# Two attention bursts joined into one, four pairs of loads of v reordered, and one difference of h taken later, in a retention and bilinear FFN kernel

## The chip, the cores and the metric

The kernel runs on one core of one Trainium2 chip. The metric is the device time of one execution in microseconds (us); the number that counts is the median over several executions. The profiler records one further execution, and its times are given from the first instruction of that execution (the span's start).

## What is computed

A linear attention with a decay per head (retention), and behind it a feed-forward layer with a product of two branches. The inputs are float32; the kernel works in bfloat16 with sums in float32.

```python
B, H, S, D = 4, 8, 768, 64
gamma = 1 - 2 ** (-5 - arange(H))
for t in range(S):
    state = gamma * state + einsum('bhd,bhe->bhde', k[:, :, t], v[:, :, t])
    y[:, :, t] = einsum('bhd,bhde->bhe', q[:, :, t], state) / sqrt(D)
x = y.transpose(0, 2, 1, 3).reshape(B * S, H * D)         # 3072 x 512
out = ((x @ w_a) * (x @ w_b)) @ w_out                     # 512 -> 1536 -> 512
```

## The kernel before

**Slots.** The attention is done in chunks of 128 positions, called slots: 24 of them, six to a batch. For one slot `t` the decay is multiplied into k and q (`scaled`, one operation each on POOL for slots 6 and up), both go through a transposing DMA on SP's queue (`flip`, L300), `scores(t)` multiplies them on TensorE in quarters of 64 x 64, VectorE multiplies the causal mask on (`aT`, L333), `update(t)` adds the slot to the running state in PSUM and a copy of it goes to `gst`, `inter(t)` multiplies the state with q, `intra(t)` the masked scores with v, and `leave(t)` copies the output y of a pair of slots to `xt` on ScalarE (L386). `turn(new, old)` writes such a burst down: scores and update for the slots `new` and `new+1`, and inter, intra and leave for `old` and `old+1`; either can be None. If both are given, the scores of `new+1` take two of the three "ff" banks of PSUM, else they take the banks y0 and y1.

**Tiles.** The FFN takes tokens in tiles J of 4, 2, 2, 2, 2, 4 and 8 slots. For tile J and each of twelve blocks `ft` of 128 hidden columns, `ffn_a` multiplies x with w_a (four matmuls, L522; ScalarE copies the result to `asb`, L525) and `ffn_g` with w_b (four matmuls, L534; VectorE multiplies `asb` on and writes `ht`, L536). `blocks(J, a, b)` does a and g in turn, `three(J, ft)` does three a's and then three g's. `a` and `g` use the three "ff" banks in rotation: a bank can be written again when its copy or product is through. The third step, h times w_out, is done by a Strassen-Winograd scheme of seven products on sums and differences `hs1` to `hs4` of quarters of `ht`. `single(J, A, B, C)` writes the seven products (`p1` to `p7`, L638) down with the first three blocks of the next tile between them, and A, B, C name the PSUM banks of its three accumulators. `hsum(J, s, a, b, eng)` makes one such sum for the blocks a to b (and a+6 to b+6); `hsums` makes the sums 2, 1 and 4.

**Order.** The order of all work is written out by hand: `seq` chains the instructions of each engine in the order in which the program makes them, and so does SP's queue with its DMAs. `casts(t)` is the step that brings a slot in: on POOL it scales k and q (and converts v, unless t is 12 to 19, whose v ScalarE converts in `v_cast`), and on SP's queue it issues `flip(t)` and then the loads of slot t+2. `load_slot(t)` issues k, then q (for a pair of slots at once, at the even one), then v. `store()` at the start of each block issues the output DMAs held until then, on the same queue.

**Sums of the sixth tile.** Tile 5 has four slots, and its sums are made in pieces: `WHEN` says behind which block which are made. A name such as "346" is sum 3 of blocks 4 to 6. Behind blocks 5 to 7 they run on VectorE, behind 8 and later on POOL.

```python
def turn(new, old, eng=nc.scalar):
    ...
    if new is not None:
        if two or old is None:
            update(new, eng)
        scores(new + 1, "y" if old is None else "ff")
        scores(new, "at")
    if old is not None:
        inter(old)
        inter(old + 1)
    ...
```

Of the kernel before, what the change touches and what calls it, by code (L numbers as in the profile page):

```python
# [16 lines left out]
PAIRS = 3  # L17


LOADS = "p0 p1 w0 w1 a1 b1 a2 k2 q2 b2 v2 o0 o1 o2 o3 o4 o5 s6 t8".split()  # L20


@with_exitstack
def kernel(
# [10 lines left out]
    nc = tc.nc  # L35
# [7 lines left out]
    NFT = DFF // P  # L43
    NSLOT = B * NCH
# [49 lines left out]
    def seq(bi):  # L94
        ins = bi.ins
        prev = last.get(ins.engine)
        if prev is not None:
            tc.add_manual_dep(ins, prev.name, nosync, reason="program order")
        last[ins.engine] = ins
        return bi  # L100
# [4 lines left out]
    def load_slot(t, names="kqv"):  # L105
        b, ci = divmod(t, NCH)
        for nm in names:
            src = {"k": k, "q": q, "v": v}[nm]
            if nm == "q":
                if t % 2 == 0:  # L110
                    load_two(nm, src, b, ci // 2, t)
                continue
            if t % 2 == 0:
                whole[nm] = raw.tile([P, 2, H, D], F32, tag=nm + "f", name=nm + "f")
            raws[nm, t] = whole[nm][:, t % 2]
            s = src[b, :, ci * P : (ci + 1) * P, :].rearrange("h p d -> p h d")
            seq(nc.sync.dma_start(out=raws[nm, t], in_=s))
# [5 lines left out]
    def load_two(nm, src, b, u, t):  # L123
        f = raw.tile([P, H, 2, D], F32, tag=nm + "f", name=nm + "f")
        s = src[b, :, 2 * u * P : 2 * (u + 1) * P, :].rearrange("h (p two) d -> p h two d", two=2)
        seq(nc.sync.dma_start(out=f, in_=s))  # L126
        for par in range(2):
            raws[nm, t + par] = f[:, :, par, :]
# [25 lines left out]

    pending = list(LOADS)

# [78 lines left out]
    def cast(engine, dst, src):  # L235
        if engine is nc.scalar:
            seq(nc.scalar.copy(dst, src))
        else:
            seq(engine.tensor_copy(dst, src))  # L239
# [29 lines left out]
    def scaled(eng, t, i):  # L269
        tab = tabs[0] if i else tabs[1 if t < 2 * PAIRS else 2]  # L270
        dst, src, tab = kqb[t][:, i], raws["kq"[i], t], tab[:, t % NCH]
        if t < 2 * PAIRS:
            dst, src = (x.rearrange("p (hp r) d -> p hp r d", r=2) if x is src else x
                        for x in (dst, src))
            tab = tab.rearrange("p (hp r) o -> p hp r o", r=2).to_broadcast([P, HP, 2, D])
        else:
            dst = dst.rearrange("p hp r d -> p r hp d")
            src = src.rearrange("p (r hp) d -> p r hp d", r=2)
            tab = tab.rearrange("p (r hp) o -> p r hp o", r=2).to_broadcast([P, 2, HP, D])
        seq(eng.tensor_tensor(dst, src, tab, op=ALU.mult))  # L280

    def new_nat(t):
        kqb[t] = nat.tile([P, 2, HP, 2, D], BF16, tag="kqb", name="kqb")
        kb[t], qb[t] = kqb[t][:, 0], kqb[t][:, 1]
        vb[t] = nat.tile([P, H, D], BF16, tag="vb", name="vb")

    def casts(t):
        new_nat(t)
        scaled(nc.gpsimd, t, 0)
        scaled(nc.gpsimd, t, 1)  # L290
        if t not in range(12, 20):
            cast(nc.gpsimd, vb[t], raws["v", t])
        flip(t)
        if t + 2 < NSLOT:
            load_slot(t + 2)

    def flip(t):
        if t % 2 == 0:
            kqT[t // 2] = tra.tile([P, 2, 2, HP, P], BF16, tag="kqT", name="kqT", bufs=3)
        seq(nc.sync.dma_start_transpose(  # L300
            out=kqT[t // 2][:, t % 2].rearrange("p a b c -> p (a b) c"),
            in_=kqb[t].rearrange("p a hp r d -> p (a hp r d)")))
# [19 lines left out]
    def scores(t, where):  # L322
        at = score_banks(where)
        for hp in range(HP):
            for c in range(2):
                for r in range(2):
                    seq(nc.tensor.matmul(at[r][half(c), hp, :],  # L327
                                         kqT[t // 2][half(r), t % 2, 0, hp, half(c)],
                                         kqT[t // 2][half(r), :, 1, hp, half(t % 2)],
                                         start=True, stop=True, skip_group_check=True))  # L330
        aT[t] = tra.tile([P, 2, HP, P], BF16, tag="aT", name="aT")
        for r in range(2):
            seq(nc.vector.tensor_tensor(aT[t][:, r], at[r], mask.to_broadcast([P, HP, P]), op=ALU.mult))  # L333
        psff.back(*at)

    def update(t, eng):
        ci = t % NCH
        if ci == NCH - 1:
            return
        if ci == 0:  # L340
            state[0] = psst.tile([P, HP, D], F32, tag="st", name="st")
        st = state[0]
        for hp in range(HP):
            for r in range(2):
                seq(nc.tensor.matmul(st[half(r), hp, :], kb[t][:, hp, r, :],  # L345
                                     vb[t][:, HP * r + hp, :],
                                     start=(ci == 0 and hp == 0), stop=(hp == HP - 1),
                                     skip_group_check=True))
        cast(eng, gst[(t + 1) % 4], st)
# [39 lines left out]
    def turn(new, old, eng=nc.scalar):  # L389
        if old is not None:  # L390
            ys[old // 2] = [psat.tile([P, 2, 2, 2, P // 2], F32, tag=f"y{r}", name="y") for r in range(2)]
        two = new is not None and (new + 1) % NCH < NCH - 1
# [8 lines that stand above are left out]
        if two:  # L401
            update(new + 1, nc.scalar)
        elif new is not None and old is not None:
            update(new, eng)
        if old is not None:
            intra(old)
            intra(old + 1)
            leave(old)
# [130 lines left out]
    def ffn_ab(J, ft):  # L539
        store()  # L540
        ffn_a(J, ft)
        ffn_g(J, ft)
# [53 lines left out]
    def hsum(J, s, a, b, eng=nc.vector):  # L596
        U = slice(int(J == 0), 2 if isinstance(J, tuple) else TILES[J] // 2)
        hs_tile(J, s)
        v = ht[J].rearrange("p (k j) (u r n) -> p r k j u n", k=2, r=2, n=P)
        A11, A12, A21, A22 = (v[:, r, k2, a:b, U] for r in range(2) for k2 in range(2))  # L600
        S = {x: hs[J, x][:, a:b, U] for x in (1, 2, 3, 4) if (J, x) in hs}
        x, y, op = {3: (A11, A21, ALU.subtract), 2: (A22, S[3], ALU.subtract), 1: (A21, A22, ALU.add),
                    4: (A12, S.get(2), ALU.subtract)}[s]
        tt(S[s], x, y, op, eng)

    def hsums(J, a, b, eng):
        for s in (2, 1, 4):
            hsum(J, s, a, b, eng)

    WHEN = {5: ["302"], 6: ["324"], 7: ["346", "202"], 8: ["102", "402"], 9: ["224", "124"],  # L610
            10: ["424"], 11: ["246", "146", "446"]}

    def sums(J, ft, eng=nc.vector):
        for what in WHEN.get(ft, []):
            hsum(J, *map(int, what), eng)

    class Group:

# [84 lines left out]
    FF = (psff, "ff")  # L703
    Y0, Y1, AT0, AT1 = ((psat, x) for x in ("y0", "y1", "at0", "at1"))
    ST = (psst, "st")

    def single(J, A, B, C):
        g = Group(J, 0, A, B, C)
        g.p1()
        g.p7()  # L710
        g.p2()
        ffn_ab(J + 1, 0)
        g.p6()
        ffn_ab(J + 1, 1)
        g.p5()
        ffn_ab(J + 1, 2)
        g.p3()
        g.p4()
# [239 lines left out]
    V_ = nc.vector  # L958

    def blocks(J, a, b):  # L960
        for ft in range(a, b):
            ffn_ab(J, ft)
            if J == 5 and ft + 1 < b:
                sums(J, ft, G_ if ft > 8 else nc.vector)

    def three(J, ft):
        store()
        for f in range(ft, ft + 3):
            ffn_a(J, f)
        for f in range(ft, ft + 3):  # L970
            ffn_g(J, f)

    def v_cast(t):
        cast(nc.scalar, vb[t], raws["v", t])
# [26 lines left out]
    hsum(2, 3, 0, 6, G_)  # L1001
    blocks(2, 6, 7)
    turn(8, None)
    three(2, 7)
    hsums(2, 0, 3, G_)
    casts(12)
    turn(None, 8)
    blocks(2, 10, NFT)
    hsums(2, 3, 6, G_)
    casts(13)  # L1010
    single(2, Y0, AT0, FF)
    casts(14)
    blocks(3, 3, 4)
    turn(10, None, V_)
    three(3, 4)
    hsum(3, 3, 0, 6, G_)
    v_cast(12)
    blocks(3, 7, 8)
    v_cast(13)
    blocks(3, 8, 9)  # L1020
    casts(15)
    hsums(3, 0, 3, G_)
    blocks(3, 9, 10)
    turn(12, 10)
# [74 lines left out]
```

## Time and profile before

| | us |
|---|---|
| median of 3 runs | 221.0 (220.89 to 221.03) |
| profiled execution, its own time | 221.23 |
| its span, first to last instruction | 219.5 |
| busy: TensorE (PE) | 212.4 |
| busy: GpSimd (POOL) | 142.1 |
| busy: VectorE (DVE) | 139.1 |
| busy: ScalarE (ACT) | 99.3 |

The profiled execution is 0.2 us above the median, and 1.7 us of its time lie outside the span. The granted TensorE clock is full throughout. In a row of the timeline stand the start, the length (both in us), the engine, the line, the operation, what is written and read, how many instructions were merged, and in brackets the idle time before the row with what ended it. The length of a TensorE row runs over the start of the next one, because matmuls overlap; the distance between two starts is what counts. SPq is the sequencer of SP issuing DMAs.

### The profile page before, as it was taken

What the parts mean: (1) busy time and instruction counts of PE and PEld (TensorE: products, weight loads), DVE (VectorE), ACT (ScalarE), POOL (GpSimd) and SP (SyncE); (2) the same over time, 40 slices, a digit from 0 to 9 for tenths busy, and PEclk for the clock granted to TensorE, in tenths of its full rate; (3) what the DMA queues carried; (4) which work ended last, traced back from release to release, by engine and by line L of the source; (5) the groups of instructions that cost most, each with busy time, mean ns of one, the idle gap of its engine ahead of it and who ended that gap; (6) DMA issues with size and microseconds to landing.
All of it is one profiled execution on the core that took longest, in us unless ns stands there. A gap on an engine that the chain in (4) does not pass through costs nothing.

```text
span 219.5 us, 5638 instructions
## 1 busy us (share of the span) xinstructions
PE 212.4 (97%) x2242; PEld 143.6 (65%) x2242; DVE 139.1 (63%) x254; ACT 99.3 (45%) x217; POOL 142.1 (65%) x163
## 2 busy tenths in 40 slices
PE   7789999999999999999999999999999999999994
PEld 3457445687458888888888655456865444448883
DVE  3776346846783463675477246986595787789642
ACT  3256325343234453455576345445545656642331
POOL 5266876778444659669675958999999975520000
PEclk9999999999999999999999999999999999999999
DMA  6999999999999995999999999960022000000055
GB/s 168 290 323 367 384 315 358 379 244 247 221 243 232 275 201 131 217 191 281 174 220 239 218 170 227 266 61 3 4 85 106 0 1 3 0 0 1 27 191 167
DMA packets 85146, 39.68 MB, mean 181 GB/s; under 512 B 57472, under 2 KB 78848, under 8 KB 85120
## 3 DMA queue, kind: packets, MB, share of 16 engines
q1 hardware_dynamic: 84976, 39.26, 76.4%
q8 instruction: 17, 0.28, 0.6%
q10 hardware_dynamic: 144, 0.07, 0.1%
q14 instruction: 9, 0.07, 0.1%
HBM read 28.31 MB, written 6.29 MB: 158 GB/s over the span
## 4 chain that ended last, share of the span: by engine, by line
PE 89%; SPq 3%; DMA 3%; issue 1%; DVE 1%; POOL 0%; ACT 0%; DVEq 0%
PE a L522 19%; PE g L534 19%; PE mA L638 12%; PE uA L778 8%; PE mB L638 6%; PE o L559 5%; PE uB L778 4%; SPq L126 3%; DMA wsta<-in_moe_w_a_dram 3%; PE mC L638 3%; PE at L327 2%; PE uC L778 2%; PE y L375 2%; PE ka L837 2%; PE kb L837 2%; PE st L345 1%
## 5 line engine op out<-in xcount | busy, mean ns | idle before, releaser
L536 DVE TENSOR_TENSOR ht<-g,asb 128x256 bf16<-128x256 f32 (+1 forms) x74 | 36.9, 502 | 37.0 <-PE g L534 32.3
L522 PE MATMUL a<-xt,wa_bf 128*128 128x256 bf16 (+1 forms) x296 | 52.4, 304 | 0.4 <-DVE ht L536 0.2
L534 PE MATMUL g<-xt,wb_bf 128*128 128x256 bf16 (+1 forms) x296 | 52.2, 304 | 0.0
L525 ACT CAST asb<-a 128x256 bf16<-128x256 f32 (+1 forms) x74 | 32.4, 437 | 39.2 <-PE a L522 37.1
L534 PEld LDWEIGHTS <-wb_bf 128*128 128x128 bf16 x296 | 28.6, 98 | 12.6
L522 PEld LDWEIGHTS <-wa_bf 128*128 128x128 bf16 x296 | 27.9, 98 | 13.0 <-DVE xt L239 0.7
L280 POOL TENSOR_TENSOR kqb<-kf,ktab 128x512 bf16<-128x512 f32 x22 | 23.1, 1056 | 16.3 <-DMA kf<-in_k_dram 10.7
L638 PEld LDWEIGHTS <-hs 128*128 128x128 bf16 x240 | 23.3, 98 | 3.9
L333 DVE TENSOR_TENSOR aT<-at,mask 128x512 bf16<-128x512 f32 x36 | 22.3, 681 | 0.3
L784 ACT COPY snap<-uA 128x512 f32<-128x512 f32 x30 | 16.7, 588 | 12.6 <-PE uA L778 12.6
L280 POOL TENSOR_TENSOR kqb<-qf,qtab 128x512 bf16<-128x512 f32 x18 | 19.3, 1071 | 3.0 <-DMA qf<-in_q_dram 3.0
L645 ACT COPY snaps<-mA 128x256 f32<-128x256 f32 x30 | 11.2, 374 | 19.8 <-PE mA L638 19.7
L572 POOL TENSOR_TENSOR hs<-ht,hs 128x384 bf16<-128x384 bf16 (+1 forms) x17 | 16.6, 983 | 5.3 <-DVE ht L536 5.3
L638 PEld LDWEIGHTS <-ht 128*128 128x128 bf16 x180 | 17.5, 98 | 2.8
L572 POOL TENSOR_TENSOR ht<-gsb,asb 128x512 bf16<-128x512 bf16 x12 | 13.6, 1158 | 6.3 <-DVE gsb L572 6.3
L572 POOL TENSOR_TENSOR hs<-ht 128x384 bf16<-128x384 bf16 (+2 forms) x12 | 13.8, 1153 | 4.2 <-DVE ht L536 4.2
L638 PE MATMUL mA<-wsum,hs 128*128 128x256 bf16 x120 | 15.7, 273 | 0.0
L239 POOL CAST vb<-vf 128x512 bf16<-128x512 f32 x16 | 10.3, 657 | 7.5 <-DMA vf<-in_v_dram 7.0
L572 DVE TENSOR_TENSOR osb<-mB,snaps 128x256 f32<-128x256 f32 x20 | 8.4, 422 | 9.1 <-PE mB L638 4.7
L386 ACT CAST xt<-y 128x512 bf16<-128x512 f32 x18 | 9.7, 589 | 2.3 <-PE y L375 2.2
L559 PE MATMUL o<-wo_bf,ht 128*128 128x512 bf16 x48 | 10.7, 379 | 0.0
L572 DVE TENSOR_TENSOR gsb<-uB,snap 128x512 bf16<-128x512 f32 x10 | 6.9, 686 | 4.2 <-ACT snap L784 2.6
(104 smaller groups left out, 327.2 us busy)
## 6 DMA issues: line engine op xcount, KB each, us to landing
qf<-in_q_dram SPq DMA_DIRECT2D x12, 512.0 KB, 5.7
out_dram<-osb SPq DMA_DIRECT2D x21, 256.0 KB, 4.1
kf<-in_k_dram SPq DMA_DIRECT2D x18, 256.0 KB, 4.3
vf<-in_v_dram SPq DMA_DIRECT2D x18, 256.0 KB, 5.2
wsta<-in_moe_w_a_dram SPq DMA_DIRECT2D x6, 512.0 KB, 7.7
wstb<-in_moe_w_b_dram SPq DMA_DIRECT2D x6, 512.0 KB, 8.0
wsto<-in_moe_w_out_dram SPq DMA_DIRECT2D x6, 512.0 KB, 8.9
kf<-in_k_dram SPq DMA_DIRECT2D x3, 512.0 KB, 7.1
```

The source lines that it names most:

```text
L280: seq(eng.tensor_tensor(dst, src, tab, op=ALU.mult))
L333: seq(nc.vector.tensor_tensor(aT[t][:, r], at[r], mask.to_broadcast([P, HP, P]), op=ALU.mult))
L522: seq(nc.tensor.matmul(a, wa_bf[:, kt, fs], xcols(J, kt, c0, c1), start=(kt == 0), stop=(kt == KT - 1)))
L525: seq(nc.scalar.copy(asb, a))
L534: seq(nc.tensor.matmul(g, wb_bf[:, kt, fs], xcols(J, kt, c0, c1), start=(kt == 0), stop=(kt == KT - 1)))
L536: seq(nc.vector.tensor_tensor(ht[J][:, ft, c0:c1], g, asbs.pop((J, ft, c0)), op=ALU.mult))
L559: seq(nc.tensor.matmul(o, ht[J][:, ft, i * P : (i + 1) * P], wo_bf[:, ft], start=(ft == 0), stop=(ft == NFT - 1), skip_group_check=True))
L572: seq(eng.tensor_tensor(dst, x, y, op=op))
L638: seq(nc.tensor.matmul(m, w, right[:, j], start=(first and j == 0), stop=(j == NP - 1), skip_group_check=True))
L645: seq(nc.scalar.copy(self.snaps[:, n], self.bank["A"]))
L778: seq(nc.tensor.matmul(m, w, right[:, k], start=(first and k == 0), stop=(k == 1), skip_group_check=True))
L784: seq(nc.scalar.copy(self.snaps[n], self.bank["A"]))
```

## The change

- The burst `turn(None, 8)` and the burst `turn(10, None, V_)` become one `turn(10, 8)`, which stands behind block 10 of tile 2, ahead of the seven products of tile 2. `update(10)` thereby comes behind the inter products, and the copy of its state is on ScalarE and no longer on VectorE. The `three(3, 4)` that followed the second burst becomes plain blocks.
- `single(2)` has Y1 as its second accumulator's bank and no longer AT0.
- For the slots 12 to 19, v of the even slot is no longer loaded behind q of that slot but behind k of the odd slot, so it stands behind the next transposing DMA in SP's queue.
- `casts(12)` moves ahead of three blocks and of the sums `hsums(2, 0, 3)`; `casts(15)` moves ahead of `hsum(3, 3, 0, 6)`.
- Sum "202" of tile 5 is made behind block 9 and no longer behind block 7, still on VectorE; "402", which reads it, is made behind block 10 and no longer behind block 8, on POOL as before.

```diff
+V_LATE = range(12, 20)
@@ casts
-        if t + 2 < NSLOT:
-            load_slot(t + 2)
+        u = t + 2
+        if u in V_LATE:
+            load_slot(u, "kq")
+            if u % 2:
+                load_slot(u - 1, "v")
+                load_slot(u, "v")
+        elif u < NSLOT:
+            load_slot(u)
@@ sums of tile 5
-    WHEN = {5: ["302"], 6: ["324"], 7: ["346", "202"], 8: ["102", "402"], 9: ["224", "124"],
-            10: ["424"], 11: ["246", "146", "446"]}
+    WHEN = {5: ["302"], 6: ["324"], 7: ["346"], 8: ["102"], 9: ["202d", "224", "124"],
+            10: ["402", "424"], 11: ["246", "146", "446"]}
@@
-            hsum(J, *map(int, what), eng)
+            hsum(J, *map(int, what[:3]), nc.vector if what[3:] else eng)
@@ the written order
     turn(8, None)
+    casts(12)
     three(2, 7)
     hsums(2, 0, 3, G_)
-    casts(12)
-    turn(None, 8)
-    blocks(2, 10, NFT)
+    blocks(2, 10, 11)
+    turn(10, 8)
+    blocks(2, 11, NFT)
     hsums(2, 3, 6, G_)
     casts(13)
-    single(2, Y0, AT0, FF)
+    single(2, Y0, Y1, FF)
     casts(14)
-    blocks(3, 3, 4)
-    turn(10, None, V_)
-    three(3, 4)
+    blocks(3, 3, 6)
+    casts(15)
     hsum(3, 3, 0, 6, G_)
+    blocks(3, 6, 7)
     v_cast(12)
     blocks(3, 7, 8)
     v_cast(13)
     blocks(3, 8, 9)
-    casts(15)
     hsums(3, 0, 3, G_)
     blocks(3, 9, 10)
     turn(12, 10)
```

## The prediction

> **What bounds the kernel now.** I read the page first: busy time and the chain of work that ended last. Then the busy time by stretches.
>
> ```profile
> PE 212.4 (97%) x2242; PEld 143.6 (65%) x2242; DVE 139.1 (63%) x254; ACT 99.3 (45%) x217; POOL 142.1 (65%) x163
> PE 89%; SPq 3%; DMA 3%; issue 1%; DVE 1%; POOL 0%; ACT 0%; DVEq 0%
> 60.00:155.00 95.00, 94.70 (x1267) 70.13 (x1264) 56.17 (x107) 46.27 (x107) 71.59 (x76) 1.00 1.02 195
> ```
>
> TensorE is the chain. In the 95 us around everything changed here, it counts 94.70 us busy at full clock. So a microsecond saved on another engine is worth nothing by itself; what counts is a shorter stream of matmuls or one of the few places where the stream waits. Busy time hides those, since matmul rows overlap. I therefore read the PE timeline by the distance between starts and compared like with like.
>
> ```profile
> 78.65 1.47 PE L534 MATMUL g<-xt,wb_bf 128*128 128x256 bf16 x12
> ...
> 80.97 0.61 PE L522 MATMUL a<-xt,wa_bf 128*128 128x256 bf16 x4
> ...
> 81.86 0.60 PE L522 MATMUL a<-xt,wa_bf 128*128 128x256 bf16 x4
> 82.37 0.60 PE L534 MATMUL g<-xt,wb_bf 128*128 128x256 bf16 x4
> ...
> 90.45 0.60 PE L534 MATMUL g<-xt,wb_bf 128*128 128x256 bf16 x4
> ...
> 91.80 1.48 PE L522 MATMUL a<-xt,wa_bf 128*128 128x256 bf16 x12
> 93.12 1.47 PE L534 MATMUL g<-xt,wb_bf 128*128 128x256 bf16 x12
> 94.68 0.60 PE L522 MATMUL a<-xt,wa_bf 128*128 128x256 bf16 x4
> ...
> 116.63 0.60 PE L534 MATMUL g<-xt,wb_bf 128*128 128x256 bf16 x4
> 117.16 0.73 PE L327 MATMUL at<-kqT 64*64 64x128 bf16 x32
> ...
> 118.74 0.61 PE L522 MATMUL a<-xt,wa_bf 128*128 128x256 bf16 x4
> ...
> 119.63 0.82 PE L638 MATMUL mA<-wo_bf,ht 128*128 128x256 bf16 x6
> 120.28 0.82 PE L638 MATMUL mB<-wsum,hs 128*128 128x256 bf16 x6
> ...
> 135.85 0.62 PE L375 MATMUL y<-aT,vb 128*64 128x128 bf16 x16
> 136.40 1.04 PE L522 MATMUL a<-xt,wa_bf 128*128 128x512 bf16 x4
> ...
> 142.76 0.62 PE L375 MATMUL y<-aT,vb 128*64 128x128 bf16 x16
> 143.57 1.02 PE L522 MATMUL a<-xt,wa_bf 128*128 128x512 bf16 x4 [0.19 <-DVE ht L536]
> ```
>
> The undisturbed pace: twelve matmuls of 256 columns take 93.12 - 91.80 = 1.32 us, four take 0.44. Three waits stand out against it: 94.68 where 93.12 + 1.32 = 94.44 was due (0.24); 82.37 where 81.86 + 0.44 was due (0.07); and 0.81 from the last product of a burst to the next block at 142.76, where the burst at 135.85 needs 0.55 (0.26).
>
> **Term 1, two bursts in one: -0.24 us.** `turn(None, 8)` takes from the end of the twelve g's to the next a: 80.97 - 78.65 - 1.32 = 1.00. `turn(10, None)`: 91.80 - 90.45 - 0.44 = 0.91. The burst that the change writes exists already: `turn(16, 14)` has the same position in its batch (slots 16 and 10 are both fifth, so one update and no second), the same banks and the same order. It takes 118.74 - 116.63 - 0.44 = 1.67. So 1.91 becomes 1.67. The matmuls are the same; what goes is three of six changes between full-array, 64x64 and 128x64 matmuls, 0.08 each. The Trainium skill (TensorEngine Tiling (Array Packing), Tiling Modes, Key Properties) says that a change of tiling mode drains TensorE, and another page of it (TensorE: Matmul & The Clock Gate, Single matmul latency) puts a drain at about 175 ns. By these, three changes would be an estimated 0.52 and the whole sum 0.28 us larger. The trace has the whole burst, so I stay with 0.24.
>
> **Term 2, the wait at 94.68: -0.24 us.** Behind the second burst VectorE is late.
>
> ```profile
> 79.36 1.30 DVE L536 TENSOR_TENSOR ht<-g,asb 128x256 bf16<-128x256 f32 x3
> ...
> 91.50 0.41 DVE L239 CAST gst<-st 128x256 bf16<-128x256 f32 x1
> 91.83 2.47 DVE L333 TENSOR_TENSOR aT<-at,mask 128x512 bf16<-128x512 f32 x4
> 94.22 1.07 DVE L536 TENSOR_TENSOR ht<-g,asb 128x256 bf16<-128x256 f32 x3
> ...
> 117.70 2.48 DVE L333 TENSOR_TENSOR aT<-at,mask 128x512 bf16<-128x512 f32 x4
> ```
>
> The copy of the state and four masks hold it till 94.22, the first of three products then ends at 94.64, and the fourth block's a, which needs that bank, starts at 94.68. With no burst there the wait has no cause. What is late next: the same pattern stays behind `turn(8, None)`, with the products from 79.36. Block 10 is then due at about 78.65 + 1.32 = 79.97 and needs the bank of the first product, free at about 79.36 + 0.43 = 79.79: 0.18 in hand. Behind the joined burst the masks fall as at 117.70 to 120.18, and there the stream runs 118.74, 119.63 (two times 0.44 later), 120.28 without a wait.
>
> ```profile
> 118.74 1.07 ACT L386 CAST xt<-y 128x512 bf16<-128x512 f32 x2
> ```
>
> The first of the seven products needs y0, the second now y1: the two copies to xt end at about 119.3 and 119.8, the products start at 119.63 and 120.28. That is 0.3 and 0.5 in hand; the copy of the state moves to ScalarE, idle at that point of the model burst. If the copies came later, the price would be 1:1.
>
> **Term 3, the wait at 82.37: -0.07 us.** It is a g waiting for the bank of an a whose copy stands behind the two copies to xt. Now only block 11 stands behind the burst before the products, as at 118.74 to 119.63, where no such wait is.
>
> **Term 4, the sum taken later: -0.26 us.**
>
> ```profile
> 140.74 0.99 DVE L572 TENSOR_TENSOR hs<-ht 128x512 bf16<-128x512 bf16 x1
> 141.65 1.26 DVE L572 TENSOR_TENSOR hs<-ht,hs 128x512 bf16<-128x512 bf16 x1
> 142.84 0.68 DVE L536 TENSOR_TENSOR ht<-g,asb 128x512 bf16<-128x512 f32 x1
> ...
> 147.29 0.69 DVE L536 TENSOR_TENSOR ht<-g,asb 128x512 bf16<-128x512 f32 x1 [0.79 <-PE g L534]
> ...
> 148.84 0.64 PE L327 MATMUL at<-kqT 64*64 64x128 bf16 x32
> ```
>
> The row at 141.65 is sum 202. Without it, the product at 142.84 starts about 1.1 earlier, ends by 142.5, and the a that waits for its bank is due at 142.76 + 0.55 = 143.31. The sum goes into the idle 0.79 us before 147.29. It may take 0.99, as the sum ahead of it, or 1.26 as here; then the product at 147.29 ends 0.2 to 0.5 late, at 148.45 at most, and the bank it frees is next written by the scores at 148.84: 0.4 in hand. Its reader 402 sits on POOL behind two other sums and loses nothing.
>
> **The DMA queue: no term, but the one that had to hold.** Slots 10 and 11 are multiplied ten microseconds earlier: block 10 from 79.97, two times 0.44, and 0.09 to the first score (as from 117.07 to 117.16) make 80.9, where the old burst came behind 90.45 + 0.44. The transpose of slot 11:
>
> ```profile
> 72.76 1.04 POOL L280 TENSOR_TENSOR kqb<-qf,qtab 128x512 bf16<-128x512 f32 x1
> ...
> 73.62 1.73 SPq L117 DMA_DIRECT2D vf<-in_v_dram  x1
> 75.47 2.89 SPq L300 DMA_TRANSPOSE kqT<-kqb  x1
> ...
> 80.37 0.92 POOL L572 TENSOR_TENSOR hs<-ht,hs 128x384 bf16<-128x384 bf16 x1 [2.64 <-DVE ht L536]
> ```
>
> And its time to landing, from the view of that tile with this one DMA in the window, then the same over all 18 transposes of the kernel:
>
> ```profile
> DMA to landing us min/median/max: 4.8/4.8/4.8
> ```
> ```profile
> DMA to landing us min/median/max: 3.1/4.9/6.6
> ```
>
> It was issued at 75.47, behind v of slot 12, and landed 4.8 later, at 80.3. Its input is ready at 73.8, and v no longer stands ahead of it: it is issued between 73.8 and 75.5 and lands between 78.6 and 80.3. I take the middle, 79.4, since a later issue into a less crowded queue gains part of its lead; even 80.3 leaves 0.6 in hand. The other three transposes of odd slots also lose a load ahead of them. v of slot 12, now behind that transpose and one load of k, is read only behind block 6 of tile 3. `casts(12)` fills the 2.64 us in which POOL is idle ahead of its sums at 80.37, where its two operations of 1.04 fit.
>
> **Sum.** -0.24 - 0.24 - 0.07 - 0.26 = -0.81 us: the profiled 221.23 becomes 220.4, the median of 221.0 becomes 220.2.
>
> **Rivals.** For the second: POOL at the sums of tile 3, and the product that reads sum 2.
>
> ```profile
> 95.04 1.64 POOL L572 TENSOR_TENSOR hs<-ht 128x768 bf16<-128x768 bf16 x1 [1.48 <-DVE ht L536]
> 96.91 1.05 POOL L280 TENSOR_TENSOR kqb<-kf,ktab 128x512 bf16<-128x512 f32 x1 [0.23 <-DMA kf<-in_k_dram]
> ...
> 103.80 0.82 PE L638 MATMUL mA<-wsum,hs 128*128 128x256 bf16 x6
> ```
>
> 1. *Transpose of slot 11 late (slower).* One mechanism: TensorE stands at the first score of the joined burst until it has landed, and everything behind shifts. It costs from a landing after 80.9, and makes the kernel slower by 0.2% (0.44 us) from 80.9 + 0.81 + 0.44 = 82.2. For it: the margin shrinks from ten microseconds to between 0.6 and 1.5. Against: all transposes landed within 3.1 to 6.6 us of issue, and 73.8 + 6.6 = 80.4. Landing at 82.4 would give 221.5. Chance 0.07.
>
> 2. *POOL held up at casts(15).* It now stands ahead of the sums of tile 3 and waits for k of slot 15, which arrived at 96.9. If it came no earlier, the two operations would last till 99.0 as before, the big sum (1.64, at 95.04 before) till 100.6, and four smaller ones, 0.9 each as at 80.37 (the three first halves and the second half of sum 2), till 104.2. The product that reads it stood at 103.80 and is then due at 103.80 - 0.55 = 103.25, its second half 0.33 later: some 0.6 late. Against: `casts(12)` and `casts(13)` run earlier, so its load is issued about a microsecond or more earlier, without v ahead. A microsecond earlier takes the price away. At 0.5 to 0.6 of it: 220.7. Chance 0.10.
> 3. *The sum hurts in its new place.* POOL runs sums there without a pause. The Trainium skill (GPSIMD Engine Reference, Specifications) says that POOL contends with VectorE when VectorE has two SBUF inputs, as this sum has. The trace leaves room: it took 1.26 beside POOL's work, and the stream waits only from about 1.65. Twice 1.26 would cost 0.9 and undo all: 221.1. Chance 0.04.
> 4. *One wait comes back elsewhere* (a copy on ScalarE behind the joined burst, a mask product): one of terms 2 and 4 is lost, 220.45. Chance 0.09.
>
> **Numbers.** The forecast has 0.70, and 220.2 is its time. The cases above leave 220.7 at the top; at the bottom the spread of the runs. Range 219.95 to 220.75. A difference of 0.2% (0.44 us) is about what a measurement of this kernel can tell from none. Faster by more: the forecast, rival 4 and part of rival 2, 0.83. Within: 0.10. Slower: rival 1, 0.07.
>
> **What would show it.** PE: one burst of about 1.67 us from 80.8, none near 91, an even pace where the waits at 82.37, 94.68 and 143.57 were. The transpose of slot 11 landing before 80.9. Sum 202 between the products behind blocks 9 and 10, under 1.65 long. Wrong if the row of the first score shows idle time ended by a DMA, or if a row mA, mB of tile 3 waits for POOL.

## The result: 0.28% faster, and the profile after

| | before | changed |
|---|---|---|
| median of 9 runs, us | 220.96 (220.78 to 221.11) | 220.34 (220.13 to 220.53) |
| profiled execution, us | 221.23 | 220.34 |
| its span, us | 219.5 | 218.6 |

The ratio is 0.9972, with a 95% interval of 0.9963 to 0.9981: 0.62 us less in the median (0.42 to 0.82 by that interval), 0.89 us less from one profiled execution to the other.

The PE timeline of the changed kernel, around the joined burst (line numbers are 7 higher than before: a is L529, g L541, scores L334, the seven products L645):

```profile
78.60 1.47 PE L541 MATMUL g<-xt,wb_bf 128*128 128x256 bf16 x12
79.91 0.60 PE L529 MATMUL a<-xt,wa_bf 128*128 128x256 bf16 x4
80.34 0.60 PE L541 MATMUL g<-xt,wb_bf 128*128 128x256 bf16 x4
80.87 0.73 PE L334 MATMUL at<-kqT 64*64 64x128 bf16 x32
...
82.45 0.61 PE L529 MATMUL a<-xt,wa_bf 128*128 128x256 bf16 x4
...
83.34 0.82 PE L645 MATMUL mA<-wo_bf,ht 128*128 128x256 bf16 x6
83.99 0.82 PE L645 MATMUL mB<-wsum,hs 128*128 128x256 bf16 x6
...
93.16 0.60 PE L529 MATMUL a<-xt,wa_bf 128*128 128x256 bf16 x4
93.60 0.60 PE L541 MATMUL g<-xt,wb_bf 128*128 128x256 bf16 x4
94.04 0.60 PE L529 MATMUL a<-xt,wa_bf 128*128 128x256 bf16 x4
```

The burst takes 82.45 - 80.34 - 0.44 = 1.67 us. Blocks and products follow at the even pace (0.44 for four matmuls, 0.65 for six), and where the second burst and its wait were, at 91 to 95, there is nothing but blocks. The transpose of slot 11, in the timeline of SP's queue, with its time to landing from the view of its tile:

```profile
73.66 2.80 SPq L307 DMA_TRANSPOSE kqT<-kqb  x1
```
```profile
DMA to landing us min/median/max: 5.6/5.6/5.6
```

It landed at 79.2, 1.6 us ahead of the first score. Term 4 in the DVE and PE timelines:

```profile
140.20 1.23 DVE L579 TENSOR_TENSOR hs<-ht 128x512 bf16<-128x512 bf16 x1
141.35 0.68 DVE L543 TENSOR_TENSOR ht<-g,asb 128x512 bf16<-128x512 f32 x1
...
145.28 0.41 DVE L579 TENSOR_TENSOR hs<-ht,hs 128x512 bf16<-128x512 bf16 x1
```
```profile
142.12 0.62 PE L382 MATMUL y<-aT,vb 128*64 128x128 bf16 x16
142.67 1.04 PE L529 MATMUL a<-xt,wa_bf 128*128 128x512 bf16 x4
```

The a behind the burst starts 0.55 after the products, with no wait. Sum 202, now at 145.28, takes 0.41 where it took 1.26.

### The profile page after: what moved, and what is told of

It is laid out like the page before. It is cut to its first block, busy times and chain, and to the rows that moved or that the text cites. A ratio compares the mean times of both kernels' runs of the same rounds, so it can differ in the third digit from the quotient of the medians.

```text
span 218.6 us, 5641 instructions
## 1 busy us (share of the span) xinstructions
PE 211.6 (97%) x2242; PEld 143.6 (66%) x2242; DVE 138.9 (64%) x253; ACT 99.5 (46%) x218; POOL 142.1 (65%) x163
## 4 chain that ended last, share of the span: by engine, by line
PE 90%; SPq 4%; DMA 4%; POOL 0%; issue 0%; DVE 0%; ACT 0%
PE g L541 19%; PE a L529 19%; PE mA L645 12%; PE uA L785 8%; PE mB L645 6%; PE o L566 5%; PE uB L785 4%; DMA wstb<-in_moe_w_b_dram 4%; SPq L127 3%; PE mC L645 3%; PE at L334 2%; PE uC L785 2%; PE y L382 2%; PE st L352 2%; PE ka L844 2%; PE kb L844 2%
## 5 line engine op out<-in xcount | busy, mean ns | idle before, releaser
L529 PE MATMUL a<-xt,wa_bf 128*128 128x256 bf16 (+1 forms) x296 | 52.7, 305 | 0.1
L541 PE MATMUL g<-xt,wb_bf 128*128 128x256 bf16 (+1 forms) x296 | 52.5, 304 | 0.2 <-POOL wb_bf L240 0.2
L541 PEld LDWEIGHTS <-wb_bf 128*128 128x128 bf16 x296 | 28.6, 98 | 12.8 <-POOL wb_bf L240 0.3
L529 PEld LDWEIGHTS <-wa_bf 128*128 128x128 bf16 x296 | 28.0, 98 | 12.2 <-POOL wa_bf L240 0.4
L645 PEld LDWEIGHTS <-hs 128*128 128x128 bf16 x240 | 23.4, 98 | 3.9
L645 PEld LDWEIGHTS <-ht 128*128 128x128 bf16 x180 | 17.5, 98 | 2.8
L645 PE MATMUL mA<-wsum,hs 128*128 128x256 bf16 x120 | 15.7, 273 | 0.0
```

The source lines that it names most:

```text
L529: seq(nc.tensor.matmul(a, wa_bf[:, kt, fs], xcols(J, kt, c0, c1), start=(kt == 0), stop=(kt == KT - 1)))
L541: seq(nc.tensor.matmul(g, wb_bf[:, kt, fs], xcols(J, kt, c0, c1), start=(kt == 0), stop=(kt == KT - 1)))
L645: seq(nc.tensor.matmul(m, w, right[:, j], start=(first and j == 0), stop=(j == NP - 1), skip_group_check=True))
```

## The experiments

Each gives a median beside the kernel before on the same chip, whose medians were 220.91 to 220.99. Differences to the changed kernel are to its 220.34, measured in another set of runs. The intervals of most ratios reach 0.2 to 0.4 us to either side, so a difference of 0.1 or 0.2 us between medians is a hint and no more.

**Sums 202 and 402 back where they were.**

```diff
-    WHEN = {5: ["302"], 6: ["324"], 7: ["346"], 8: ["102"], 9: ["202d", "224", "124"],
-            10: ["402", "424"], 11: ["246", "146", "446"]}
+    WHEN = {5: ["302"], 6: ["324"], 7: ["346", "202"], 8: ["102", "402"], 9: ["224", "124"],
+            10: ["424"], 11: ["246", "146", "446"]}
```

> The changed kernel with sums 202 and 402 where they were before (behind blocks 7 and 8). Theory (term 4): VectorE is late again ahead of the burst of slots 20 and 18, the a behind it waits about 0.26 us, and the kernel takes 0.26 us more than the changed one: about 220.6. Rival (the gain lies in the joined burst alone): no difference, 220.34, and no idle time in front of that a.

Measured: 220.49 (220.14 to 221.29), ratio to before 0.9972 (0.9957 to 0.9986). That is 0.15 above the changed kernel in the median and nothing in the fastest run (220.14 against 220.13); the interval allows nothing as well as 0.26. The profiled execution (220.92) shows why, in its DVE, POOL and PE timelines:

```profile
140.66 0.41 DVE L579 TENSOR_TENSOR hs<-ht 128x512 bf16<-128x512 bf16 x1
140.99 0.42 DVE L579 TENSOR_TENSOR hs<-ht,hs 128x512 bf16<-128x512 bf16 x1
141.78 0.69 DVE L543 TENSOR_TENSOR ht<-g,asb 128x512 bf16<-128x512 f32 x1 [0.37 <-PE g L541]
```
```profile
141.08 1.23 POOL L281 TENSOR_TENSOR kqb<-kf,ktab 128x512 bf16<-128x512 f32 x1 [0.82 <-DMA kf<-in_k_dram]
```
```profile
81.52 0.64 PE L334 MATMUL at<-kqT 64*64 64x128 bf16 x32 [0.52 <-DMA kqT<-kqb]
```

Here the two sums took 0.41 and 0.42, where they took 0.99 and 1.26 before: POOL stood idle for 0.82 us, waiting for a load, and its next instruction began only at 141.08. VectorE was not late and no wait of 0.26 arose. POOL before the change, at the same place:

```profile
140.41 1.04 POOL L280 TENSOR_TENSOR kqb<-kf,ktab 128x512 bf16<-128x512 f32 x1
141.41 1.22 POOL L280 TENSOR_TENSOR kqb<-qf,qtab 128x512 bf16<-128x512 f32 x1
```

Those two end at 141.45 and 142.63, the two sums of before at 140.74 + 0.99 = 141.73 and 141.65 + 1.26 = 142.91: each sum ends 0.28 after the POOL instruction that was running when it began. By these two profiles term 4 hangs on the phase between the two engines in that microsecond, and that on when a load lands. The last row is something else: the joined burst waits for the transpose of slot 11. That is rival 1, in a kernel whose program up to there is that of the changed one. TensorE waits 0.52 us there in this execution, so not all of the 0.15 need be term 4. The transpose, issued at 76.39, landed at 81.5:

```profile
74.90 0.96 SPq L127 DMA_DIRECT2D qf<-in_q_dram  x1
76.39 2.28 SPq L307 DMA_TRANSPOSE kqT<-kqb  x1
```
```profile
DMA to landing us min/median/max: 5.1/5.1/5.1
```

**The sums alone, on the kernel before.** The same edit in the other direction.

> The kernel before with only the sums 202 and 402 moved. Theory (the four terms add up without touching each other): 0.26 us less than before, 220.7, with the waits at 82.4 and 94.7 still there. Rival (the sum hurts in its new place, beside POOL's sums): no gain, 220.96 or more, with sum 202 over 1.65 us long.

Measured: 220.88 (220.71 to 221.07) against 220.99, ratio 0.9986 (0.9974 to 0.9999): 0.11 us in the median, less than half of the 0.26, as from the other side. The interval, 0.02 to 0.57 us, does not rule out 0.26. In the profiled execution (220.94) the a behind the burst comes 0.54 after the products, with no wait.

**v in the old order.**

```diff
-V_LATE = range(12, 20)
+V_LATE = range(0, 0)
```

> The changed kernel with v of the slots 12 to 19 loaded in the old order, ahead of the next transpose. Theory: the transpose of slot 11 lands about 0.9 us later, at about 80.1, still ahead of the first score at 80.9, so no change there: 220.34, within 0.1. Rival (the order of v is what lets the bursts be joined): TensorE waits at the joined burst, or at the burst of slots 16 and 14, whose transpose landed only 0.3 us ahead of its use in the changed kernel; 0.3 to 0.9 us more, up to 221.2, with idle time in front of the scores ended by a DMA.

Measured: 220.86 (220.18 to 222.0), ratio 0.9986 (0.9967 to 1.0006). Three of the 11 runs (220.18 to 220.26) are as fast as the changed kernel; the median is 0.5 worse. The rival holds. PE timeline of its profiled execution (221.44), and the landing:

```profile
80.51 0.60 PE L541 MATMUL g<-xt,wb_bf 128*128 128x256 bf16 x4
82.08 0.64 PE L334 MATMUL at<-kqT 64*64 64x128 bf16 x32 [0.97 <-DMA kqT<-kqb]
```
```profile
76.29 3.45 SPq L307 DMA_TRANSPOSE kqT<-kqb  x1
```
```profile
DMA to landing us min/median/max: 5.7/5.7/5.7
```

The transpose landed at 82.0, and the score came 1.04 us later than 80.51 + 0.44 + 0.09 = 81.04. So in most executions the gain of the joined burst hangs on the order of the loads.

**Three loads ahead of the transpose of slot 11.** The changed kernel with

```diff
+            if u == 12:
+                load_slot(12)
+                load_slot(13)
```

in `casts`, so that v of slot 12 and k and v of slot 13 are issued ahead of it.

> The changed kernel with v of slot 12 and k and v of slot 13 loaded ahead of the transpose of slot 11. Theory (rival 1 of the prediction has a slope of one to one from 80.9): three loads of about 0.9 us each push the landing from 79.2 to about 82, TensorE waits about 1.1 us at the first score, and the kernel takes that much more than the changed one: about 221.4. Rival (the transpose does not queue behind the loads ahead of it): landing before 80.9 and no change, 220.34.

Measured: 223.34 (221.63 to 225.05), ratio 1.0105 (1.0054 to 1.0156). PE timeline of its profiled execution (222.04):

```profile
82.65 0.64 PE L338 MATMUL at<-kqT 64*64 64x128 bf16 x32 [1.75 <-DMA kqT<-kqb]
```

The direction and the place are as the theory has them; the wait is 1.8 and not 1.1 us. The median lies between two groups of three runs: 221.63 to 222.04, to which this profile belongs, 1.3 to 1.7 above the changed kernel, and 224.64 to 225.05, where the granted clock was 0.992 against 0.999 to 1.0. For the second group there is no profile; its cause stays open.

**k and q of slot 12 behind the transpose too.**

```diff
-            load_slot(u, "kq")
+            if u > 12:
+                if u == 13:
+                    load_slot(12, "kq")
+                load_slot(u, "kq")
...
-    casts(12)
     three(2, 7)
     hsums(2, 0, 3, G_)
+    casts(12)
```

> The changed kernel with k and q of slot 12 also loaded behind the transpose of slot 11, and the step that brings in slot 12 back behind the sums 2, 1 and 4 of tile 2 (which by itself changed nothing at the joined burst). Theory (the transpose lands anywhere from 79.2 to 81.5 in different executions, since 0.75 MB of loads stand ahead of it, and TensorE waits where it is past 80.9): it now lands about 2.5 us earlier, 76.7 to 79, no execution waits there, and the median falls to the fastest executions of the changed kernel, 220.15 to 220.25, with no run above 220.5 from this cause. Rival (the landing follows the input's end on POOL, not the loads ahead): still 79 to 81, median 220.34 and the same spread.

Measured: 220.39 (220.13 to 221.20), ratio 0.9975 (0.9966 to 0.9985). The transpose does as expected, issued at 74.32 and landed at 77.8, three microseconds ahead of use:

```profile
74.32 1.23 SPq L310 DMA_TRANSPOSE kqT<-kqb  x1
```
```profile
DMA to landing us min/median/max: 3.5/3.5/3.5
```

The median does not fall, and single runs still reach 221.20. So the late landing at the joined burst is not what holds the changed kernel's median at 220.34; by this, most of its executions don't wait there.

**The bursts apart again.** `turn(None, 8)`, `turn(10, None, V_)`, `three(3, 4)` and AT0 as before, the rest as changed.

```diff
-    blocks(2, 10, 11)
-    turn(10, 8)
-    blocks(2, 11, NFT)
+    turn(None, 8)
+    blocks(2, 10, NFT)
...
-    single(2, Y0, Y1, FF)
+    single(2, Y0, AT0, FF)
...
-    blocks(3, 3, 6)
+    blocks(3, 3, 4)
+    turn(10, None, V_)
+    three(3, 4)
     casts(15)
     hsum(3, 3, 0, 6, G_)
-    blocks(3, 6, 7)
```

> The changed kernel with the two bursts apart again where they were, and three a's then three g's behind the second one; the loads, the other moved steps and sum 202 stay as changed. Theory (terms 1 to 3): 0.24 + 0.24 + 0.07 = 0.55 us more than the changed one, about 220.9, with the waits at 82.4 and 94.6 back. Rival (the skill's price of a drain, 175 ns each): 0.83 us more, 221.2. Rival (earlier loads alone took the waits away): 0.24 us more, 220.6, with no wait at 94.6.

Measured: 220.92 (220.82 to 221.10), ratio 0.9991 (0.9978 to 1.0005), so 0.58 above the changed kernel where terms 1 to 3 have 0.55. Both waits are back: 82.21 - 81.69 = 0.52 where 0.44 is the pace, and 94.52 - 92.95 - 1.31 = 0.26.

```profile
81.69 0.60 PE L529 MATMUL a<-xt,wa_bf 128*128 128x256 bf16 x4
82.21 0.60 PE L541 MATMUL g<-xt,wb_bf 128*128 128x256 bf16 x4
...
92.95 1.47 PE L541 MATMUL g<-xt,wb_bf 128*128 128x256 bf16 x12
94.52 0.60 PE L529 MATMUL a<-xt,wa_bf 128*128 128x256 bf16 x4
```

This kernel is the one with the sums alone (220.88, same kernel before) plus the new order of loads and the two moved steps. The two lie 0.04 us apart: without the joined burst, no gain from these is seen.

**The price of a change of tiling.** Two full-array matmuls of the identity matrix `ident` by itself into an idle bank, in six bursts, once between update and intra and once ahead of the burst.

```diff
+    def probe():
+        ...
+        for n in range(2):
+            seq(nc.tensor.matmul(bank[:, n * P : (n + 1) * P], ident, ident, start=True, stop=True,
+                                 skip_group_check=True))
```

> The changed kernel with two added full-array matmuls of 128 columns, whose result nobody reads, inside each of the six bursts from slots 12 and 10 on, between the update and the intra products (both 128x64): two more changes of tiling per burst, 12 in all. Theory (0.08 us for each change, from the joined burst): 6 x 2 x 0.053 + 12 x 0.08 = 1.6 us more than the changed kernel, 221.9. Rival (a drain of 175 ns each): 0.64 + 2.1 = 2.7 us more, 223.1.

> The changed kernel with the same two added matmuls ahead of each of those six bursts, behind full-array matmuls, so that no change of tiling is added. Both theories: 6 x 2 x 0.053 = 0.64 us more, 221.0. What the one with the matmuls inside takes beyond this is the price of 12 changes of tiling.

Measured: 222.31 (222.09 to 222.33) inside, 221.10 (220.96 to 221.30) ahead. The difference is 1.21 us for 12 changes, 0.10 each, somewhat over the 0.08 of the joined burst and well under 0.175. These are changes from 128x64 to the full array and back. The runs price such a change as a whole and do not show what it consists of.

**casts(12) and casts(15) back.** Each stands again behind the sums that it stood behind before the change.

> The changed kernel with the steps that bring in slots 12 and 15 back behind the sums they were behind before. Theory: POOL has idle time enough in either order, no change: 220.34, within 0.1. Rival (POOL's order carries part of the gain): the second half of sum 2 of tile 2 or the transposes of slots 15 to 17 come late, 0.2 us or more above, with idle time on TensorE in front of a product or a score.

Measured: 220.25 (220.23 to 220.92), ratio 0.9971 (0.9960 to 0.9982). The median is that of the changed kernel or a little less; 4 of 11 runs are above 220.5. Its profiled execution (220.62) shows the transpose of slot 17 late at the burst of slots 16 and 14:

```profile
116.89 0.64 PE L334 MATMUL at<-kqT 64*64 64x128 bf16 x32 [0.42 <-DMA kqT<-kqb]
```

Its sum 202, in the new place, meets a POOL instruction, and again ends 0.28 behind it (146.73 and 146.45); TensorE's pace there stays even:

```profile
145.29 1.16 POOL L579 TENSOR_TENSOR hs<-ht 128x512 bf16<-128x512 bf16 x1
```
```profile
145.57 1.16 DVE L579 TENSOR_TENSOR hs<-ht,hs 128x512 bf16<-128x512 bf16 x1
```

**Three further waits taken out.** The burst of slots 12 and 10 one block later; behind the burst of 14 and 12, one copy to xt and one mask later; FF and ST exchanged in the first group of tile 5.

```diff
-    blocks(3, 9, 10)
+    blocks(3, 9, 11)
     turn(12, 10)
-    blocks(3, 10, NFT)
+    blocks(3, 11, NFT)
...
-    turn(14, 12)
+    turn(14, 12, hold=True)
...
+    ffn_a(4, 6)
+    leave(12, (1,))
+    ffn_g(4, 6)
+    late.pop()()
...
-        a, b = Group(5, 0, ST, AT0, FF), Group(5, 1, FF, AT1, FF)
+        a, b = Group(5, 0, FF, AT0, ST), Group(5, 1, FF, AT1, FF)
```

> The changed kernel with three more edits against the waits that its trace still shows: the burst of slots 12 and 10 one block later, ahead of block 11; behind the burst of slots 14 and 12 the second copy to xt behind block 6's a and the last mask behind block 6's g; and the first accumulator of the first group of the sixth tile in an ff bank, the third in the bank of the state. Theory: the waits of 0.08 at 99.7, 0.08 + 0.12 at 113.1 to 113.8 and 0.08 at 149.3 go, 0.36 us less than the changed kernel: about 220.0. Rival (a wait removed comes back at the next late bank): 220.2 to 220.34, with new idle time within 3 us behind those places.

Measured: 220.07 (219.94 to 220.19), ratio 0.9959 (0.9945 to 0.9972). Behind the burst of 14 and 12 the pace is now even:

```profile
111.96 0.61 PE L537 MATMUL a<-xt,wa_bf 128*128 128x256 bf16 x4
112.41 0.60 PE L549 MATMUL g<-xt,wb_bf 128*128 128x256 bf16 x4
112.84 0.60 PE L537 MATMUL a<-xt,wa_bf 128*128 128x256 bf16 x4
113.28 0.60 PE L549 MATMUL g<-xt,wb_bf 128*128 128x256 bf16 x4
113.72 0.60 PE L537 MATMUL a<-xt,wa_bf 128*128 128x256 bf16 x4
```

0.27 us in the median of the 0.36 forecast. This profiled execution waits 0.23 us for the transpose of slot 11:

```profile
81.14 0.64 PE L336 MATMUL at<-kqT 64*64 64x128 bf16 x32 [0.23 <-DMA kqT<-kqb]
```

**Both together.** The three edits, the two loads behind the transpose, and with these `casts(12)` behind the sums.

> The same move of the two loads together with the three edits against the remaining waits. Theory (the gains add up): 0.36 us below the fastest executions of the changed kernel, a median of 219.8 to 219.9. Rival (another late transfer or bank takes the place of the waits): 220.07 or more, as with the three edits alone.

Measured: 220.05 (219.78 to 220.08), ratio 0.9953 (0.9942 to 0.9965): 0.89 us below the kernel before (220.94), and in the median no better than the three edits alone, so the forecast 219.8 to 219.9 was not reached.

## Why the prediction was right, point by point

**Terms 1 to 3 (0.55 us) held.** The joined burst takes the forecast 1.67 us, the waits at 82.4 and 94.7 are gone, none came back beside them, and undoing these edits alone costs 0.58. The model burst (slots 16 and 14) was the right row to price it from. By the figure of the Trainium skill (TensorE: Matmul & The Clock Gate, Single matmul latency) it would have been an estimated 0.28 more; 12 added changes measure 0.10 each.

**Term 4 (0.26 us) is the term that looks mis-sized.** The mechanism is right, but its size was read from one execution. The 1.26 was no duration of the sum, which takes 0.41: it was a wait for POOL's scaling. So the working that without the sum the product "starts about 1.1 earlier" holds for the phase of that execution alone; in the profile with the sums put back the two sums cost VectorE 0.41 and 0.42 and TensorE nothing. (Even there it would have been 0.97: with the sums alone moved, the product comes 1.14 behind the start of its g, for which it waits, and 140.73 + 1.14 = 141.87. The wait goes in either case.) How many executions have the wait was not measured. The medians put the term at 0.11 to 0.15, which would make the forecast sum of 0.81 into 0.66 to 0.70, near the measured 0.62; but the intervals of these two runs hold 0.26 as well, and that of the result reaches 0.82. So the size of term 4 stays open between nothing and 0.26. The profiled execution of before lay 0.27 above its median of 9 runs; that this is the same wait is likely but not shown.

**Rival 1 (the transpose of slot 11) came true in part.** The first score is due at about 80.9, and it waited about one to one behind a landing at 81.1 (0.23), 81.5 (0.52), 82.0 (0.97) and 82.6 (1.75). What I missed is that a landing read from one execution is a sample. In six profiles with the joined burst and the changed order of v it was at 79.2, 79.8, 80.5, 80.6, 81.1 and 81.5, two of them too late; 79.2 and 81.5 are of the same program up to there. That the changed kernel's own profile has 79.2, beside the forecast 79.4, is therefore partly luck. The bound of 73.8 + 6.6 = 80.4 failed at its first number, since the issue itself came at 76.39 with the sums put back: k of slot 11 and everything behind it ran over a microsecond late. Its second number is no bound either: the same transpose took 7.2 to landing with the sums alone moved. And by the prediction's own slope a landing at 82.4 gives 220.2 + 1.5 = 221.7, not 221.5. The wait shows in single executions and not in the median.

**The order of v** I had put down as no term. By itself it is none, but the joined burst needs it: without it the median is 220.86, and most of the gain is gone.

**Rivals 2, 3 and 4** did not come. POOL's sums of tile 3 were in time with `casts(15)` ahead of them, and putting both steps back changes no median. The sum in its new place took 0.41 in the changed kernel's profile and at most 1.16, inside the 1.65 of room that the prediction read. No wait came back, though the measured time lies near the 220.45 of rival 4.

**Open:** the spread of the changed kernel with the transpose out of the way (220.13 to 221.20), of which one candidate was seen once, the transpose of slot 17 at 116.9 (in the changed kernel's profile it landed 7.4 after its issue, only 0.3 ahead of use); how much term 4 is worth; and the upper half of the runs with three loads ahead.

## What to carry to other kernels

Where one engine is the chain and its rows overlap, compare distances between starts against the undisturbed pace; waits of 0.07 to 0.26 us that no busy share shows then become terms of the forecast. Price a rewritten stretch from a place in the same trace where the new shape already stands. A wait whose length hangs on another engine's timing or on a transfer's landing is a sample from one execution: weigh it by how often its cause can recur, and give a transfer that a change brings close to its use a margin for the spread of its queue, here over two microseconds.

## What the runs showed of the hardware that I had not expected

- A sum of two bf16 operands on VectorE (128x512) takes 0.41 us; where it begins while an elementwise instruction of POOL is running, it ends 0.28 after that one's end instead. In the thirteen profiles this holds for all 38 such sums between 137 and 147 (0.27 to 0.29). In the changed kernel:

```profile
140.10 1.04 POOL L281 TENSOR_TENSOR kqb<-kf,ktab 128x512 bf16<-128x512 f32 x1
...
144.10 1.15 POOL L579 TENSOR_TENSOR hs<-ht 128x512 bf16<-128x512 bf16 x1
145.45 1.26 POOL L579 TENSOR_TENSOR hs<-ht,hs 128x512 bf16<-128x512 bf16 x1 [0.20 <-DVE ht L543]
```

  The sum at 140.20 began 0.1 after POOL's scaling and ended at 141.43, 0.29 behind its end at 141.14; the one at 145.28 fell into POOL's pause between 145.25 and 145.45 and took 0.41. The POOL instruction that follows such a sum is longer in turn (1.22 after 1.04 before the change). The Trainium skill (SBUF — State Buffer, SBUF: two separate sides) says that the port pair which the two engines share is locked for a whole instruction, by whichever starts first, between a POOL operation that reads SBUF and a VectorE operation with two SBUF inputs. The traces agree, except that the sum ends 0.28 and not 0.41 behind POOL's instruction, so part of its time is not blocked. In the kernel with two loads behind the transpose the sum was first by 0.01, took its 0.41, and POOL's scaling took 1.30 where it takes 1.04:

```profile
140.03 0.41 DVE L582 TENSOR_TENSOR hs<-ht 128x512 bf16<-128x512 bf16 x1
```
```profile
140.04 1.30 POOL L281 TENSOR_TENSOR kqb<-kf,ktab 128x512 bf16<-128x512 f32 x1
```

  No run varied this by itself.
- The same transposing DMA, behind the same DMAs, landed 2.3 us apart in two executions (79.2 and 81.5), with 5.6 and 5.1 us from issue to landing: the delay came ahead of its issue (73.66 and 76.39).
- A change between full-array and 128x64 matmuls cost about 0.10 us on TensorE (12 added changes), the three changes between full-array, 64x64 and 128x64 matmuls that the joined burst saves 0.08 each.
